# A gated linear-attention and GEGLU kernel: two neighbouring tokens in a partition instead of one

## The chip, the cores and the metric

The kernel runs on one core of a Trainium2 chip. The metric is the device time of one execution in microseconds (us). Five engines run their own instruction queues in order: PE (TensorE, matrix products), DVE (VectorE), ACT (ScalarE), POOL (GpSimd) and SP (SyncE, which here only issues transfers). PEld is PE's loading of weights, which the profile keeps apart. POOL issues transfers too, on a queue of its own (q0); SP's queue is q1. Sixteen DMA engines carry out the transfers of both.

## The reference

There are 4 batches of 8 heads, with 768 tokens of 48 elements, in fp32. For each batch and head a state `S` (48x48, complex) is carried from token to token: it is multiplied by a decay per row, and the outer product of `k` and `v` is added. `y` is `q` times the state's real part.

```
mag = sqrt(a_re^2 + a_im^2);  scale = min(mag, 0.999) / (mag + 1e-6)
for t in range(768):
    S = (a_re + i a_im)[t] * scale[t] * S  +  k[t] v[t]^T
    y[t] = q[t] . Re(S)
x = y as (3072 tokens, 384)
out = x + sigmoid(x @ w_res) * ((gelu(x @ w_gate) * (x @ w_val)) @ w_out)
```

The four weight matrices are 384x1536, 384x1536, 1536x384 and 384x384.

## The kernel before

The tokens are worked on in 12 groups `p` of 256 tokens: group p holds tokens 256*(p//4) to 256*(p//4)+255 of batch p%4, all heads. Groups 0 to 3 are the first of their batch, 8 to 11 the last. A group consists of two chunks `c` of 128 tokens. In every tile a partition is one token of a chunk, and the free dimension holds chunk, head and element (`wide = [128, C, H, D]`, L233). A load (`rows`, L282; `load`, L301) fetches one chunk of one input: 128 tokens x 8 heads x 48 elements, 192 KB in runs of 192 B.

**Gates** (`gates`, L306). A complex product of decays becomes a sum of log magnitudes and a sum of angles. ACT squares both parts (SQI, SQR), DVE adds and caps them (ADD), ACT takes the logarithm (LM); the tangent of the angle is formed (LNR, EXR, TH) and its arctangent taken (ATN). The running sums over the tokens of a chunk are fp32 products on PE with a triangular matrix of ones: CSL (L352) for log magnitudes, CST (L381) for angles, one per chunk and quantity, 128x384 each. Chunk 0 uses `lmat[0]`, which counts backwards from the end of chunk 0, and chunk 1 uses `lmat[1]`; so the midpoint of the group is the reference point. ACT makes E and Ei from CSL (EX, EI). The angle in turns is reduced to its fraction (OFF on ACT, FR on DVE L388), and ACT takes sine and cosine (SIN, COS; ABS on DVE before the cosine). The angle is carried on from chunk to chunk and from group to group: POOL multiplies the last row (CRA, CRB, L424) and an accumulating transfer adds it to the next chunk's first row (CDA, CDB, L429), ahead of that chunk's CST. For groups 4 to 11 small transfers bring decays to another layout (DR, DS, DE, DI, DT), of which ML, ME, MM, MN make the factor M.

**Products and attention** (L436, L458). DVE multiplies q with E and k with Ei (QE, KE, L441) and with the cosines and sines (QR, KR, L449) into the bf16 tiles `padQ` and `padK`. For groups 0 to 4 PE transposes them (TP, L481) and ACT and DVE copy the result out (CP); for groups 5 to 11 SP issues one transposing transfer per tile (QT, KT, L454). Per chunk and half of the heads, four products give the 128x128 attention blocks (AT), and DVE multiplies them with a triangular mask (AM). DK (L502) is padK times v, summed over the tokens of a chunk; MI and ED (L524 to L532) add it to the state `G`. Y (L540, L543) takes the masked blocks times v plus the query times the state. v is loaded as fp32 (Lvf, L615) and cast to bf16 by POOL (VC, L617).

**The feed-forward part** (`unit`, L556) runs on 7 units: groups 0, 1, then pairs (2,3) to (10,11). x is transposed (XT, XC), PE forms gate and value products (GP, VP, L569), ACT applies gelu (GE), DVE multiplies (HM, L575). RP (L579) and SG give the residual gate, OP (L589) is the output product, OT (DVE, L594) and RX (POOL, L600) finish it, and SP stores it (ST, L603).

**The order.** `ORDER` (L64) is one list of step names, written out. Each engine runs its steps in this order; semaphores hold a step until its operands are there. ACT must load a table before each change of function family (`log`, `trig`, `gelu` in the list). The weights are loaded by POOL with a cast to bf16 (Wg, Wv, Wr, Wo); two small copies, HOLDW and HOLDO (L627), keep them back until given `ai` loads have landed. The number of buffers of each tile is in `PARAMS` (L16).

Of the kernel before, what the change touches and what calls it, by code (L numbers as in the profile page):

```python
# [21 lines left out]
 'bufs': {'ar': 4,  # L22
# [3 lines left out]
          'k': 4,  # L26
          'vf': 2,
          'v': 4,
# [11 lines left out]
          'qk': 2,  # L40
          'atm': 2,
# [7 lines left out]
          'padK': 2},  # L49
 'share': {'kE': 'qE'},  # L50
 'sqe': {-1: ('ACT', 'ACT')},
 'offe': {-1: 'ACT'},
 'abse': {-1: 'DVE'},
 'cpe': ('ACT', 'DVE'),
# [3 lines left out]
 'holds': {'HOLDW': ('ai', 2, 1), 'HOLDO': ('ai', 4, 1)},  # L58
 'oph': 1,
 'rese': ['POOL'],  # L60
 'resl': 'POOL',
 'vhw': [0, 1, 2, 3, 4, 5, 6, 7, 8, 9, 10, 11]}

ORDER = """  # L64
Lar0.0 log Lk0.0 Lar0.1 Lar1.0 LNR0.0 Lar1.1 SQR0.0 EXR0.0 Lai0.0 LNR0.1 SQR0.1 Lai0.1 EXR0.1 Lai1.0 SQR1 Lai1.1
SQI0.0 ADD0.0 Lvf0.0 SQI0.1 TH0.0 LM0.0 Lq0.0 ADD0.1 CSL0.0 TH0.1 LM0.1 Lar2.0 SQI1 Lq0.1 CSL0.1 ADD1 EX0.0 VC0.0
EI0.0 Lq1.0 QE0.0 EX0.1 Lar2.1 EI0.1 DE0 trig Lar3.0 QE0.1 Lar3.1 ATN0.0 ATN0.1 Lvf0.1 CST0.0 SQR2 CST0.1 Lk0.1 OFF0.0
OFF0.1 FR0.0 Lk1.0 SQR3 FR0.1 Lk1.1 ABS0.0 SIN0.1 ABS0.1 CRB0 SIN0.0 VC0.1 Lai2.0 COS0.0 COS0.1 QR0.0 Lar4.0 QR0.1 log
Lai2.1 KE0.0 KE0.1 LNR1 Lai3.0 KR0.0 KR0.1 LM1 DK0.0 Lai3.1 EXR1 TP0.0.0 Lq1.1 MI0 SQI2 TH1 TP0.0.1 HOLDW Wr Lai4.0
# [12 lines left out]
FR3.0 Lar8.0 DK1.1 FR2.1 OFF3.1 Y1.1 ED1 CDB1 SIN2 Lq2.1 OP0.1.0 FR3.1 ATN4 CRB2 ABS2 Lai6.1 ABS3 CRB3 COS2 VC2.0
Lvf2.1 OT0.1 COS3 CDB0 KR2 Lai7.0 SIN3 RX0.1 QE2 Lai7.1 DK2.0 X1.1 XC1.0 XT1.1 MI2 Lar8.1 gelu XC1.1 VC2.1 QR2 GP1.0
Lq3.0 RP1.0 SQI6 KE3 DK2.1 Lq3.1 SG1.0 RP1.1 SQI7 ED2 VP1.0 Lq4.0 KR3 GE1.0 SG1.1 GP1.1 Lk4.0 SQR7 ADD6 GP1.2 GP1.3
Lq4.1 GE1.1 HM1.0 GE1.3 ADD7 DR6 GE1.2 GP1.4 SQR8 Lvf3.0 GP1.5 GP1.6 QE3 GE1.4 GP1.7 Lk4.1 DR7 GE1.5 GP1.8 GE1.6 GP1.9
QR3 GE1.7 GP1.10 Lai8.0 GE1.8 GP1.11 GE1.9 VP1.1 GE1.10 GE1.11 Lk5.0 VP1.2 HM1.1 VP1.3 log HM1.2 VC3.0 VP1.4 Lq5.0
HM1.3 VP1.5 HM1.4 VP1.6 HM1.5 VP1.7 LM4 Lq5.1 HM1.6 VP1.8 HM1.7 VP1.9 LM5 HM1.8 VP1.10 Lk5.1 HM1.9 VP1.11 ML4 HM1.10
LNR7 CSL4.0 Lai8.1 HM1.11 TP2.0.0 LNR6 TP2.0.1 Lk6.0 CP2.0.0.1 ME4 CSL4.1 ML5 EXR6 CP2.0.1.1 Lk6.1 DK3.0 CP2.0.0.0 TH6
ST0.0 EI4.0 AT2.0.0 Lvf3.1 ME5 MI3 EX4.0 DI4 CP2.0.1.0 AM2.0.0 CSL5.0 Lar9.0 EI4.1 TP2.1.0 EX4.1 KE4 AT2.0.1 EI5.0
CSL5.1 Lar9.1 DE4 EX5.0 AM2.0.1 CST4.0 CP2.1.0.0 ST0.1 CP2.1.0.1 Lq6.0 DI5 EX5.1 TP2.1.1 EI5.1 Y2.0 CP2.1.1.1 CST5.0  # L90
EXR7 DT4.0 Lar10.0 OP1.0.0 X2.0 TH7 DT4.1 OFF5.0 Lar10.1 OFF4.0 FR5.0 DE5 CP2.1.1.0 FR4.0 AT2.1.0 trig CRA5 Lq6.1
OT1.0 AT2.1.1 XT2.0 CRA4 OP1.1.0 AM2.1.0 DT5.0 AM2.1.1 XC2.0 Lq7.0 SQR9 MM4 CDA4 MN4 Lq7.1 EN4 ATN7 Y2.1 OT1.1 VC3.1
ATN6 TP3.0.0 DT5.1 Lk7.0 TP3.0.1 X2.1 CP3.0.0.1 DK3.1 CDB2 CP3.0.0.0 CP3.0.1.1 Lvf4.0 CST4.1 ED3 EB4 XT2.1 RX1.0
CP3.0.1.0 AT3.0.0 XC2.1 Lar11.0 TP3.1.0 SQR10 AM3.0.0 CDA5 AT3.0.1 CP3.1.0.1 OFF4.1 TP3.1.1 Lk7.1 AM3.0.1 CP3.1.0.0
RX1.1 CP3.1.1.1 Y3.0 CP3.1.1.0 Lk8.0 FR4.1 AT3.1.0 CDB3 X3.0 MM5 AT3.1.1 ABS4 CST5.1 SIN4 Lvf4.1 MN5 AM3.1.0 CRB4
XT3.0 COS4 Lk8.1 DS6.1 AM3.1.1 OFF5.1 EN5 Y3.1 VC4.0 Lai9.0 XC3.0 KR4 DS7.1 X3.1 ST1.0 SQI8 FR5.1 XT3.1 Lvf5.0 DK4.0
DS7.0 XC3.1 SIN5 ABS5 GP2.0 Lai9.1 VC4.1 KE5 COS5 GP2.1 DS6.0 MI4 GP2.2 gelu CRB5 KR5 Lvf5.1 GP2.3 ADD8 DK4.1 GE2.0
Lai10.0 GE2.3 GP2.4 VC5.0 ED4 GE2.1 Lai10.1 DR8 QE4 DK5.0 GE2.2 GP2.5 GE2.4 QR4 GP2.6 SQI9 VC5.1 KT5 GP2.7 QE5 GE2.5
GP2.8 GE2.6 ADD9 GE2.7 RP2.3 GE2.8 VP2.0 Lvf6.0 QR5 DR9 SG2.3 GP2.9 HM2.0 GP2.10 Lvf6.1 GE2.9 VP2.1 GE2.10 TP4.0.0
HM2.1 RP2.1 CP4.0.0.0 CP4.0.0.1 TP4.0.1 QT5 SG2.1 RP2.2 CP4.0.1.1 CP4.0.1.0 VC6.0 VP2.2 SG2.2 GP2.11 VC6.1 HM2.2  # L100
Lvf7.0 RP2.0 GE2.11 AT4.0.0 SG2.0 VP2.3 AM4.0.0 log Lk9.0 AT4.0.1 HM2.3 VP2.4 AM4.0.1 VP2.5 Lvf7.1 LM6 HM2.4 VP2.6 LM7
Lai11.0 HM2.5 VP2.7 HM2.6 VC7.0 LNR8 ST1.1 VP2.8 Lai11.1 HM2.7 LNR9 VP2.9 HM2.8 Lvf8.0 ML6 VP2.10 EXR8 VC7.1 HM2.9
VP2.11 EXR9 HM2.10 Lq8.0 Y4.0 HM2.11 ML7 ME6 CSL6.0 ME7 EB5 Lvf8.1 TH8 X4.0 CSL6.1 EI6.0 Lq8.1 TH9 TP4.1.0 EX6.0
TP4.1.1 DI6 EI6.1 Lq9.0 CP4.1.0.1 CSL7.0 EX6.1 KE6 CP4.1.0.0 CSL7.1 Lq9.1 DE6 CP4.1.1.0 CP4.1.1.1 CST6.0 EX7.0 Lar11.1
EX7.1 AT4.1.0 DT6.0 AT4.1.1 EI7.0 AM4.1.0 CST7.0 Lk9.1 EI7.1 DT6.1 AM4.1.1 OP2.0.0 OFF6.0 Lk10.0 OFF7.0 FR6.0 DI7 trig
FR7.0 CRA6 Lk10.1 Y4.1 OT2.0 CRA7 SQR11 XT4.0 AT5.0.0 MI5 CDA6 AT5.0.1 ATN8 OP2.1.0 AM5.0.0 CDA7 XC4.0 MM6 AM5.0.1
X4.1 MN6 DT7.0 ATN9 EN6 CST6.1 OT2.1 CDB4 Y5.0 OFF6.1 XT4.1 AT5.1.0 CDB5 EB6 XC4.1 AT5.1.1 OP2.2.0 FR6.1 X5.0 DT7.1
# [62 lines left out]
def kernel(  # L170
# [111 lines left out]
    def rows(a, p, c):  # L282
        s, b = divmod(p, B)
        t0 = (s * C + c) * 128
        return a[b, :, t0:t0 + 128, :].rearrange("h t d -> t h d")
# [411 lines left out]
```

## Time and profile before

| | |
|---|---|
| three runs | 302.81, 303.13, 304.01 us; median 303.13 |
| the profiled execution | 300.27 us, span of the instructions 298.5 us |
| busy | PE 242.7, ACT 216.4, DVE 209.3, PEld 148.4, POOL 126.5 us |
| loads of q, k, v, a_re, a_im | 120, of 192 KB; landing about 4 us after issue |
| moved by DMA | 39.98 MB in 164,891 packets; 156,800 of them under 512 B |
| ACT table loads | 21 of 1.28 us |

The span runs from the first to the last instruction of the profiled execution. "Busy" is the time in which an engine has an instruction in work; where two neighbours overlap, it counts once, so it is less than the number times the mean. A group of instructions is named by its line in the kernel, its engine and `output<-inputs`; many ACT steps share line 294, a helper. `A <- B` after an idle time says that A waited, and that B came last. "x2" in a chain counts instructions merged into one row; one fp32 product on PE appears as two MATMUL records.

### The profile page before, as it was taken

Reading aid. Unit: us, or ns where it says so; the run is one execution under the profiler, and the core shown is the slowest. Engines: PE = TensorE matmul, PEld = TensorE weight load, DVE = VectorE, ACT = ScalarE, POOL = GpSimd, SP = SyncE. Lnnn points to the kernel's source line nnn. Section 1 sums busy time; section 2 is a strip of 40 time slices with the busy share of each in tenths; the row PEclk is TensorE's granted clock in tenths of the full one; section 3 lists DMA queues with packets and bytes.
Section 4 is the critical chain, followed back from the end, with each engine's and each line's share of the span. In section 5 each row is a group of like instructions: output and inputs, shape, how many; then the busy total and the mean of one; then the engine's idle time right before and its main releaser. Section 6 shows DMA issues by size and latency. Waiting matters only on the chain.

```text
span 298.5 us, 5373 instructions
## 1 busy us (share of the span) xinstructions
PE 242.7 (81%) x1896; PEld 148.4 (50%) x1896; DVE 209.3 (70%) x352; ACT 216.4 (73%) x385; POOL 126.5 (42%) x164
## 2 busy tenths in 40 slices
PE   0327468965899877699987999969999899999992
PEld 0106236643586654355664446634557445664461
DVE  1448746659887759649879988889388898641721
ACT  5889988899799859579968789656695783347120
POOL 4225414068422969610799605990019420121013
PEclk9966879999599979799999999999999999999999
DMA  7999999999999996999418993297500197020002
GB/s 153 207 198 193 187 185 168 184 200 203 199 179 226 169 187 135 200 213 187 67 28 182 167 217 67 39 157 155 93 3 3 56 194 143 0 82 26 0 29 79
DMA packets 164891, 39.98 MB, mean 134 GB/s; under 512 B 156800, under 2 KB 164864, under 8 KB 164864
## 3 DMA queue, kind: packets, MB, share of 16 engines
q1 hardware_dynamic: 157376, 35.66, 60.5%
q0 software_dynamic: 7488, 3.97, 10.4%
q8 instruction: 15, 0.25, 0.3%
q14 instruction: 12, 0.10, 0.1%
HBM read 31.33 MB, written 4.76 MB: 121 GB/s over the span
## 4 chain that ended last, share of the span: by engine, by line
PE 57%; DMA 14%; DVE 8%; issue 6%; ACT 5%; SPq 5%; POOL 4%; POOLq 0%; DVEq 0%; ACTq 0%
PE gv L569 26%; PE sums L589 12%; DMA ai<-in_a_im_dram 8%; DMA d<-m 4%; SPq L304 4%; PE sums L579 4%; PE sums L381 3%; PE sums L352 3%; PE at L494 2%; PE dk L502 2%; PE tp L481 2%; DMA ar<-in_a_re_dram 1%; DVE atm L497 1%; ACT ar L294 1%; POOL m L342 1%
## 5 line engine op out<-in xcount | busy, mean ns | idle before, releaser
L575 DVE SCALAR_TENSOR_TENSOR h<-h,gv 128x512 bf16<-128x512 bf16 (+1 forms) x84 | 47.7, 607 | 20.8 <-PE gv L569 18.3
L569 PE MATMUL gv<-xT,wg 128*128 128x512 bf16 (+1 forms) x252 | 53.9, 360 | 6.2 <-ACT h L294 3.3
L294 ACT ACTIVATE h<-gv 128x512 bf16<-128x512 f32 (+1 forms) x84 | 41.6, 543 | 17.6 <-PE gv L569 16.5
L589 PE MATMUL sums<-wo,h 128*128 128x384 bf16 x288 | 50.6, 326 | 2.4 <-ACT Ei L294 2.4
L569 PE MATMUL gv<-xT,wv 128*128 128x512 bf16 (+1 forms) x252 | 52.5, 350 | 0.0
L600 POOL TENSOR_TENSOR ot<-ot,x 128x384 f32<-128x384 f32 x24 | 26.0, 1086 | 52.3 <-DVE ot L594 49.5
L569 PEld LDWEIGHTS <-wg 128*128 128x128 bf16 x252 | 25.1, 101 | 28.6 <-issue 7.9
L589 PEld LDWEIGHTS <-h 128*128 128x128 bf16 x288 | 27.4, 98 | 20.1 <-issue 2.3
L497 DVE TENSOR_TENSOR atm<-at,mask 128x512 bf16<-128x512 f32 x48 | 31.8, 683 | 5.2 <-PE at L494 4.9
L569 PEld LDWEIGHTS <-wv 128*128 128x128 bf16 x252 | 24.4, 98 | 20.5 <-issue 0.3
L424 POOL TENSOR_SCALAR G<-m 32x384 f32<-32x384 f32 x16 | 23.5, 1470 | 16.6 <-DVE m L388 13.1
L294 ACT ACTIVATE ar<-ar 128x768 f32<-128x768 f32 (+1 forms) x35 | 28.2, 819 | 2.0 <-DMA ar<-in_a_re_dram 1.9
L664 ACT ACT_TABLE_LOAD x21 | 26.9, 1283 | 1.1 <-PEq L681 0.7
L294 ACT ACTIVATE sg<-sums 128x384 f32<-128x384 f32 x24 | 11.7, 490 | 17.8 <-PE sums L579 17.6
L617 POOL CAST v<-vf 128x384 bf16<-128x384 f32 x24 | 17.5, 733 | 16.8 <-DMA vf<-in_v_dram 15.7
L594 DVE SCALAR_TENSOR_TENSOR ot<-sg,sums 128x384 f32<-128x384 f32 x24 | 13.2, 550 | 15.9 <-PE sums L589 12.3
L363 POOL DMA_DIRECT2D d<-Ei x8 | 4.0, 494 | 47.5 <-ACT Ei L294 40.1
L502 PE MATMUL dk<-v,padK 128*96 128x48 bf16 x160 | 11.0, 209 | 15.5 <-POOL v L617 7.2
L381 PE MATMUL sums<-ai,ut 128*128 128x384 f32 x40 | 17.7, 538 | 5.2 <-ACT qk L298 1.8
L294 ACT ACTIVATE m<-sums,magic 128x384 f32<-128x384 f32 x24 | 13.6, 584 | 11.0 <-PE sums L381 10.8
L502 PEld LDWEIGHTS <-padK 128*96 128x96 bf16 x160 | 10.5, 134 | 19.6 <-DVE padK L449 9.7
L352 PE MATMUL sums<-m,lt 128*128 128x384 f32 x24 | 11.3, 555 | 10.3 <-ACT m L294 10.3
(80 smaller groups left out, 478.0 us busy)
## 6 DMA issues: line engine op xcount, KB each, us to landing
ar<-in_a_re_dram SPq DMA_DIRECT2D x24, 192.0 KB, 4.2
k<-in_k_dram SPq DMA_DIRECT2D x24, 192.0 KB, 3.9
ai<-in_a_im_dram SPq DMA_DIRECT2D x24, 192.0 KB, 3.9
vf<-in_v_dram SPq DMA_DIRECT2D x24, 192.0 KB, 3.9
q<-in_q_dram SPq DMA_DIRECT2D x24, 192.0 KB, 4.1
out_dram<-ot SPq DMA_DIRECT2D x24, 192.0 KB, 2.3
wg<-in_moe_w_gate_dram POOLq DMA_DIRECT2D x4, 288.0 KB, 11.5
wv<-in_moe_w_val_dram POOLq DMA_DIRECT2D x4, 288.0 KB, 12.9
```

The costliest lines, as they stand in the source:

```text
L294: return nc.scalar.activation(out=out, in_=in_, func=func, **kw)
L352: st.add("CSL%d.%d" % (p, c), "PE", lambda c=c: nc.tensor.matmul(out=st["csl", (p, c)], lhsT=lmat[c], rhs=part(("m2", p), (c,)), start=Tru ...
L381: st.add("CST%d.%d" % (p, c), "PE", lambda c=c: nc.tensor.matmul(out=st["cst", (p, c)], lhsT=tmat[c if s == 0 else 1], rhs=part(("ai", p), ...
L424: st.add("CR%s%d" % (nm, p), "POOL", lambda: nc.gpsimd.tensor_scalar(out=row[96:128], in0=part(("m2", p), (c,))[96:128], scalar1=-2.0 * ma ...
L497: st.add("AM" + sfx, "DVE", lambda: nc.vector.tensor_tensor(out=st["atm", i], in0=st["at", i], in1=mask4, op=OP.mult), r=[("at", i)], w=[( ...
L502: return [nc.tensor.matmul(out=d[0:DD, h * D:(h + 1) * D], lhsT=K(c * H + h), rhs=st["v", p][:, c, h], start=(c == 0 and h == 0), stop=(h ...
L569: st.add("%sP%d.%d" % (nm.upper(), u, f), "PE", lambda f=f, nm=nm, w=w: [nc.tensor.matmul(out=st[nm + "p", (u, f)][:, 0:n], lhsT=w[:, i, f ...
L575: st.add("HM%d.%d" % (u, f), "DVE", lambda f=f: nc.vector.scalar_tensor_tensor(out=st["h2", u][:, f, 0:n], in0=st["h2", u][:, f, 0:n], sca ...
L589: st.add("OP%d.%d.%d" % (u, jj, hh), "PE", lambda jj=jj, fs=fs: [nc.tensor.matmul(out=st["op", (u, jj)], lhsT=st["h2", u][:, f, jj * 128:( ...
L600: st.add("RX%d.%d" % (u, jj), rese, lambda jj=jj, pc=(p, c), eng=eng: eng.tensor_tensor(out=st["ot", (u, jj)], in0=st["ot", (u, jj)], in1= ...
L617: st.add("VC%d.%d" % (p, c), "POOL", lambda c=c: nc.gpsimd.tensor_copy(out=st["v", p][:, c], in_=st["vf", (p, c)]), r=[("vf", (p, c))], w= ...
L664: nc.scalar.preload_act_table_set(tables[nm])
```

## The change

A partition now holds two neighbouring tokens, 2i and 2i+1, of the group's 256 (`wide = [128, H, C, D]`, where C is now the parity). It comes with these edits:

- **Loads.** One transfer per group and input (384 KB, runs of 384 B) instead of two; group 0 is loaded in halves of the heads, and its gate steps are split by heads. That makes 64 loads instead of 120.
- **Sums.** SL (POOL; DVE for group 0) adds the log magnitudes of the two tokens, one CSL per group sums the pairs, and the odd token's running sum is the result. UL (DVE) subtracts the odd token's own value, which gives the even token's. SP, CST and UT (DVE) do the same for the angles. The exponentials and OFF, FR still run once per parity. The lower half of `lmat` covers partitions 0 to 63, the upper 64 to 127, so the midpoint is kept.
- **Carry.** One row copy CR (DVE) and one accumulating transfer CD per group, for groups 0 to 3 to 4 to 7 and these to 8 to 11; none within a group.
- **Chunks.** Chunk c is now partitions 64c to 64c+63 with both parities, its 128 tokens in the order even, then odd. The mask is rebuilt for that order. The transposed tiles QT, KT are `[128, C, H*C, 64]`; the transposing transfer is one per chunk, of 64 partitions, 28 instead of 14.
- **v.** One load and one cast (VC, 128x768) per group into `vb`; VS (DVE, 64x768) copies chunk 0 for groups 0 to 7. Four transfers VX per group (48 in all, 64 partitions x 768 B, SP's queue) bring v into the even-odd order that Y needs (`vp`).
- **DK.** Groups 0 to 7: per half of the heads 8 products over both chunks, whose 96 columns hold the sum up to the midpoint and the whole sum. Groups 8 to 11: 16 products over 64 partitions. MI and ED are split by halves of the heads for groups 0 to 7.
- **Stores** take 128 rows that are two tokens apart in pairs of partitions; the rows stay 1,536 B.
- **Buffers.** `ar` 4 to 3, `k` 4 to 3, `atm` 2 to 6, `v` (4) gives way to `vb` (2) and `vp` (2), `qk` goes, PSUM stays.
- **Order.** The list is written anew. HOLDW and HOLDO wait for the loads of the same groups. The casts VC0 and VC1 stand ahead of the weights on POOL's queue, VC2 ahead of HOLDO.

Cut at the first gate product of each unit (GP0.0 to GP6.0), the two lists hold these numbers of steps (before/after):

| stretch | UL+UT | VS | CR | MI+ED | QE, QR, KE, KR | EN, MM, MN | CSL+CST | ATN | SIN+COS | tables | loads | VX | KT+QT |
|---|---|---|---|---|---|---|---|---|---|---|---|---|---|
| to GP0.0 | 0/6 | 0/2 | 1/2 | 2/4 | 9/9 | 0/0 | 8/6 | 5/5 | 4/6 | 4/4 | 31/22 | 0/5 | 0/0 |
| to GP1.0 | 0/4 | 0/2 | 3/2 | 3/4 | 7/4 | 0/0 | 8/4 | 2/0 | 6/2 | 4/3 | 23/14 | 0/7 | 0/0 |
| to GP2.0 | 0/4 | 0/2 | 3/1 | 3/9 | 6/11 | 6/6 | 8/4 | 2/4 | 3/6 | 2/3 | 33/15 | 0/12 | 0/0 |
| to GP3.0 | 0/4 | 0/1 | 5/1 | 4/7 | 9/8 | 5/2 | 8/4 | 2/2 | 5/4 | 3/3 | 22/7 | 0/4 | 3/6 |
| to GP4.0 | 0/4 | 0/1 | 2/2 | 4/8 | 8/7 | 7/8 | 8/4 | 2/2 | 4/4 | 3/4 | 11/6 | 0/8 | 4/8 |
| to GP5.0 | 0/4 | 0/0 | 2/0 | 2/2 | 8/9 | 6/7 | 8/4 | 0/0 | 4/4 | 4/3 | 0/0 | 0/12 | 4/9 |
| to GP6.0 | 0/0 | 0/0 | 0/0 | 2/2 | 5/4 | 0/1 | 0/0 | 0/0 | 0/0 | 1/1 | 0/0 | 0/0 | 3/5 |

The core of the diff:

```diff
- 'bufs': {'ar': 4,
+ 'bufs': {'ar': 3,
...
+ 'sle': {-1: 'POOL', 0: 'DVE'},
+ 'ste': {-1: 'POOL', 0: 'DVE'},
+ 'vce': {-1: 'POOL'},
+ 'vse': {-1: 'DVE'},
+ 'cre': 'DVE',
...
-    wide = [128, C, H, D]
+    wide = [128, H, C, D]
...
-    def rows(a, p, c):
+    def rows(a, p, h0=0, h1=H):
         s, b = divmod(p, B)
-        t0 = (s * C + c) * 128
-        return a[b, :, t0:t0 + 128, :].rearrange("h t d -> t h d")
+        t0 = s * C * 128
+        return a[b, h0:h1, t0:t0 + C * 128, :].rearrange("h (p r) d -> p h (r d)", r=C)
...
+        st.add("SL%d%s" % (p, z), sle, lambda: vec(sle).tensor_tensor(
+            out=Pc("m2", 0), in0=Pc("m2", 0), in1=Pc("m2", 1), op=OP.add),
...
+        st.add("CSL%d%s" % (p, z), "PE", lambda: nc.tensor.matmul(
+            out=summed(("csl", p), h), lhsT=lmat, rhs=Pc("m2", 0), start=True, stop=True),
...
+        st.add("UL%d%s" % (p, z), "DVE", lambda: nc.vector.tensor_tensor(
+            out=Pc("E", 0), in0=summed(("csl", p), h), in1=Pc("m2", 1), op=OP.subtract),
...
+        for c in (1, 0):
+            for nm, n, sc in (("EI", "Ei", -0.5), ("EX", "E", 0.5)):
+                src = [("csl", p, z)] if c else [("E", p, sub(z, 0))]
...
+        st.add("UT%d%s" % (p, z), "DVE", lambda: nc.vector.scalar_tensor_tensor(
+            out=Pc("ai", 0), in0=Pc("ai", 1), scalar=-I2PI, in1=summed(("cst", p), h), op0=OP.mult, op1=OP.add),
...
+            out=G[b][96:128], in0=st["m2", p][96:128, :, 1, :], scalar1=-2.0 * math.pi, scalar2=None, op0=OP.mult),
...
+                for c in range(C):
+                    st.add(nm.upper() + "T%d.%d" % (p, c), "SP", lambda nm=nm, c=c: nc.sync.dma_start_transpose(
+                        out=st[nm.upper() + "T", p][:, c], in_=st["pad" + nm.upper(), p][c * 64:c * 64 + 64]),
...
+            st.add("VS%d" % p, vse, lambda: copy(vse, st["vb", p][0:64, :, 0], st["vb", p][0:64, :, 1]),
...
+        for j in range(2 * C):
+            c, r = divmod(j, C)
+            st.add("VX%d.%d" % (p, j), "SP", lambda c=c, r=r: nc.sync.dma_start(
+                out=st["vp", p][r * 64:r * 64 + 64, c], in_=st["vb", p][c * 64:c * 64 + 64, r, 1]),
```

## The prediction

> **What bounds the kernel now.** I read the busy times by stretch first, cut at the start of the first gate product of each of the seven units (41.3, 77.2, 122.1, 160.7, 200.6, 238.0, 267.7 us). The columns are the length, then busy time of PE, PEld, DVE, ACT, POOL, the clock, the DMA share, GB/s.
>
> ```profile
> 0.00:41.30 41.30, 16.58 (x110) 10.08 (x111) 21.46 (x41) 33.89 (x56) 15.15 (x29) 0.79 1.06 187
> 41.30:77.20 35.90, 24.95 (x221) 17.82 (x221) 24.63 (x45) 33.08 (x57) 17.79 (x23) 0.97 1.12 190
> 77.20:122.10 44.90, 37.05 (x338) 27.04 (x339) 36.85 (x66) 37.74 (x72) 25.93 (x32) 0.91 0.94 182
> 122.10:160.70 38.60, 36.24 (x293) 21.40 (x292) 29.35 (x51) 30.26 (x55) 20.08 (x26) 0.96 0.69 133
> 160.70:200.60 39.90, 36.68 (x292) 21.41 (x291) 35.47 (x56) 31.04 (x58) 25.66 (x35) 1.00 0.75 135
> 200.60:238.00 37.40, 36.03 (x272) 20.56 (x272) 28.81 (x48) 26.67 (x50) 12.65 (x15) 1.00 0.34 69
> 238.00:267.70 29.70, 29.70 (x252) 17.28 (x251) 22.01 (x34) 14.63 (x25) 4.63 (x5) 1.00 0.48 105
> 267.70:298.50 30.80, 25.49 (x134) 12.83 (x131) 10.74 (x17) 9.12 (x16) 4.56 (x5) 0.98 0.09 33
> ```
>
> The reader is to see three regimes. Up to 77.2 us the DMA engines are full (1.06 and 1.12) and ACT is busy 66.97 of 77.2 us, 87%, while PE is half idle. From 77.2 to 238.0 us PE carries the kernel: 73.3 of 83.5 us in the first two stretches, 72.7 of 77.3 in the next two, and 94% over the three from 122.1 to 238.0 (108.95 of 115.9). DVE has room there: 66.2 and 64.3 us. From 238.0 on it is PE alone, and no gate work is left.
>
> Next the longest pieces of the chain that ended last, from 28 to 78 us (start, length, what):
>
> ```profile
> 29.44 19.43 DMA ai<-in_a_im_dram
> 49.17 0.83 POOL wo L641
> 51.46 9.73 DMA d<-m
> 64.22 3.13 DMA d<-m
> ```
>
> The first is one load of 192 KB that took 19.4 us because the weights and earlier loads stood before it; a held weight load and two tiny transfers follow on POOL's queue. So the start hangs on the DMA. The page's queue part gives the packets:
>
> ```profile
> q1 hardware_dynamic: 157376, 35.66, 60.5%
> q0 software_dynamic: 7488, 3.97, 10.4%
> HBM read 31.33 MB, written 4.76 MB: 121 GB/s over the span
> ```
>
> The 120 loads are 122,880 of the packets, 192 B each. Last, the groups by line (count, then busy us and mean ns) give prices:
>
> ```profile
> L600 POOL TENSOR_TENSOR ot<-ot,x 128x384 f32<-128x384 f32 x24 | 26.0, 1086 | 52.3 <-DVE ot L594 49.5
> L424 POOL TENSOR_SCALAR G<-m 32x384 f32<-32x384 f32 x16 | 23.5, 1470 | 16.6 <-DVE m L388 13.1
> L388 DVE SCALAR_TENSOR_TENSOR m<-m,sums 128x384 f32<-128x384 f32 x24 | 12.8, 547 | 7.8 <-ACT m L294 7.8
> L352 PE MATMUL sums<-m,lt 128*128 128x384 f32 x24 | 11.3, 555 | 10.3 <-ACT m L294 10.3
> ```
>
> **Part 1, loads of 384 B.** Packets fall from 122,880 to 61,440, for the same 23.6 MB. At 187 GB/s a 192 B packet costs an engine 16 x 192 B / 187 GB/s = 16.4 ns. A 384 B packet costs between 16.4 ns (bytes free) and 32.8 ns (packets free). The nearest other row is the weights: q0 took 10.4% of 16 x 298.5 us, 497 us; with some 2,500 tiny packets at 16 ns, its 4,992 weight packets of (31.33 - 23.6) MB / 4,992 = 1,549 B read took 91.5 ns each. A line through both points gives 16.4 + 192 x 75.1 / 1,357 = 27 ns, which I take as an estimate. All loads then need 61,440 x 27 / 16 = 104 us of the DMA instead of 126; bounds 63 and 126.
>
> The Trainium skill (DMA: Bandwidth & Descriptors, Why small descriptors are slow) charges each packet a fixed few cycles beside its bytes; that agrees in kind, and its count for unaligned pieces (9 + 3 cycles on average against 14 + 3) would make it 16.4 x 17 / 12 = 23 ns, and the loads 89 us. By that the start gains some 3 us more than below.
>
> The gain is only of use up to 77.2 us, where the DMA is full. ACT is next. By the counts of steps per stretch, ACT has some 3.3 us less to do ahead of the second unit's products, because two arctangents, parts of the sines and one table load now stand behind that point: 63.6 us. At 88% busy (87% now) the second unit starts at 63.6 / 0.88 = 72.3 us, **4.9 us earlier**; the chain from the ai load through POOL, above, loses a link because the casts of v stand ahead of the small transfers. If the DMA gives nothing, this term is 0.
>
> **Part 2, one sum per group and quantity.** Each group had two sums of log magnitudes and two of angles; now one each. A pair of the L352 records (one fp32 product) takes 0.65 to 0.70 us in the chain. 24 full-width products go: 24 x 0.66 = 15.8 us of PE, 5.3 of them in each of the two double stretches between 77.2 and 238.0 us. This is PE work that was on the path, but it only counts as long as PE stays the bound.
>
> **Part 3, what DVE and POOL take over.** New on DVE: UL and UT, one of each per group, 128x384 with a PSUM operand, like L388: 12 x 2 x 0.547 = 13.1 us. VS, 8 copies of 64x768 bf16: no row; the 128x384 copy of line 299 is 0.35 us, twice that is 0.70; I take 0.5, 4 us. CR, 8 of 32x384, between 0.35 (128x384, line 401) and 0.547: I take 0.35, 2.8 us. MI and ED in halves, 0.35 each where a whole was 0.55: +2.4. SL, SP of group 0: 4 x 0.35. In all 23.7 us; overlap between neighbours (the parts sum to 5% more than the busy time) makes it 22.6, and DVE goes **from 209.3 to 232 us**, past what PE will have (242.7 - 15.8 + DK, below = 229).
>
> By stretches, with the counts of steps before and after, DVE gains 11.4 us between 77.2 and 160.7 (8 UL/UT 4.4, 3 VS 1.5, 2 CR 0.7, MI/ED +1.75, four whole products moved in 4.1, three small ones out -1.1) and 7.3 between 160.7 and 238.0 (8 UL/UT 4.4, one VS 0.5, 2 CR 0.7, the rest 1.7). With the 5% off, DVE has 66.2 + 10.8 = 77.0 us and 64.3 + 6.9 = 71.2 us there, PE 73.3 - 5.3 = 68.0 and 72.7 - 5.3 = 67.4, ACT (some 3 us moved in) 71 and 58. **DVE becomes the bound.** Whether it can be filled as PE was is the question on which the sum rests. I take PE's 94%, as the busiest engine of an order fixed by hand: 77.0 / 0.94 = 81.9 us (83.5 before) and 71.2 / 0.94 = 75.7 us (77.3 before).
>
> POOL loses 16 row copies (L424, 23.5 us) and 8 accumulating transfers (8 us) and gains 22 adds like L600 (23.9 us): lighter by 8 us, not a bound. Its adds stand in the path of each sum, 1.1 us and a hop; the carry from chunk to chunk within a group (1.2 us on POOL, 2.8 us on the DMA and one more sum) is gone from the same path. I set one against the other.
>
> **Part 4, the rest.** DK: in the first 8 groups as many products, with 96 columns instead of 48 (a 128-column transpose pair of 8 takes 0.45 us, the 8 DK products 0.50: nothing; at most double, 8 us); in the last 4 groups 8 more of half depth, 4 x 8 x 0.06 = 2 us, half of it beside idle PE time. VX: 48 moves of 48 KB within SBUF, 2.4 MB, packets of 768 B: 48 x 64 x at most 55 ns / 16 = 11 us of DMA, spread over 230 us. They wait for the cast on SP's queue, with later loads, transposes and stores queued behind them; SP already waits 9.0 us for the casts' buffers and 85 us for results to store, mostly where loads run far ahead. Nothing, unless the loads come late. Fewer buffers for ar and k: the same answer. The transposes by DMA become 28 halves. Their DMA time was 60.5% of 298.5 us less 126 for loads and some 17 for stores, 38 us for 14. It stays if it goes by bytes, doubles if by instruction; from 122 us on the DMA is 0.09 to 0.75 busy, so it hides, and each pair may land some 2 us later (an issue takes 1.3 to 3.9 us of SP).
>
> Here the Trainium skill speaks against the change (the same page, Rules for kernel authors): two transfers to partition halves serialize, one of 128 partitions is better, and under 64 KB a transfer is mostly overhead. The page of before has no half transfers. By that rule the 14 transposes and 48 moves bring 62 overheads of some 2 us, 124 us in all; taken as latency beside other work they cost nothing, and one per unit on the path would cost 7 x 2 = 14 us.
>
> **The sum.** 72.3 + 81.9 + 75.7 + 29.7 + 30.8 = 290.4 us of span (the last two stretches unchanged, the 2 us of DK against DVE's 1 us less there). 300.27 - 298.5 = 1.8 us lie around it: 292.2 us, 97.3% of the profiled execution's 300.27. The median shown is 303.13, above that execution, so I scale: 303.13 x 0.973 = **295.0 us**.
>
> **Rivals.** (a) *The loads get no faster*, at 32.8 ns: the second unit starts at 77.2, the sum is 295.3 + 1.8 = 297.1, or 299.9 on the median's scale. For it: the DMA share is full with any packet size. Against: the weights' packets move bytes faster than the loads'. 16%, and from 298 to 304. (b) *DVE is no better filled than before*, **slower**: UL, UT, VS and CR stand in DVE's fixed order between the wide products, and whoever waits for them (ACT's exponentials of the even tokens, then PE) waits for everything ahead. The point that decides is 148.2 / 165.7 = 89% of DVE's time between the second unit's start and the sixth's (160.8 us now, 165.7 with the 4.9 added); below it the start's 4.9 us are given back. DVE's best stretch now is 35.47 of 39.9, 89% too. At 87%: 72.3 + 88.5 + 81.8 + 60.5 + 1.8 = 304.9, or 307.8 us. 28%. (c) *More comes out*: the short path without a carry, half as many PSUM sum tiles held, a packet at 23 ns: start at 69, DVE at 98%: 69 + 78.6 + 72.7 + 60.5 + 1.8 = 282.6, or 285.3 us. 13%. The forecast has 43%, from 290 to 300.
>
> **The numbers.** A measurement of this kernel can tell about 0.5%, 301.6 to 304.6 us. Faster: 41 of the forecast's 43, all 13 of (c), 8 of (a): 62%. Same: 2 + 7 + 3 of (b): 12%. Slower: the remaining 25 of (b) and 1 of (a): 26%. The range for 8 in 10 goes from (c)'s centre, a little lower, to (b)'s centre, a little higher: 284 to 309.
>
> **What would show it.** In the profile after: half the load packets and over 220 GB/s in the first stretch (step 1; at 190 it is wrong); second unit at 70 to 74 us; 24 pairs of fp32 sums and PE near 229 us; DVE at 230 or more and 92 to 95% busy between the second unit and the sixth. If DVE's total stays under 225, or it idles over 10% there behind ACT or POOL, part 3 is wrong. If AT products wait for KT or QT, or Y for vp, the hidden transfers were not hidden.

## The result and the profile after

The change made the kernel **slower**: 349.85 us (median of 4 runs, 348.56 to 351.49) against 303.57 us (4 runs, 302.81 to 307.73), a ratio of 1.154 with a 95% interval of 1.147 to 1.160. The forecast was 295.0 us. The execution profiled after has a span of 346.8 us. Ratios are taken over the fast executions of both kernels, and of the kernel before these are two of seven beside runs 1 to 8 (about 295 us) but nearly all beside runs 9 to 14 (about 299), so that steps between runs are read from medians here.

Busy time by stretch, cut again at the first gate product of each unit (now at 43.4, 71.7, 117.6, 162.0, 213.6, 262.7 and 305.9 us); the columns are those of the table of before.

```profile
0.00:43.40 43.40, 15.56 (x107) 11.10 (x108) 28.09 (x65) 35.51 (x63) 18.62 (x32) 0.89 1.07 225
43.40:71.70 28.30, 23.55 (x205) 17.49 (x206) 24.43 (x49) 26.47 (x50) 12.61 (x17) 0.86 1.06 236
71.70:117.60 45.90, 32.63 (x309) 23.47 (x310) 42.91 (x77) 40.77 (x73) 25.41 (x31) 0.83 0.67 172
117.60:162.00 44.40, 37.18 (x310) 22.36 (x308) 36.49 (x61) 34.09 (x60) 14.89 (x18) 0.92 0.61 103
162.00:213.60 51.60, 39.37 (x288) 22.17 (x288) 41.08 (x68) 31.89 (x58) 22.91 (x29) 0.86 0.64 112
213.60:262.70 49.10, 39.00 (x280) 21.99 (x281) 34.95 (x54) 26.76 (x50) 15.61 (x17) 0.88 0.49 63
262.70:305.90 43.20, 34.60 (x257) 19.10 (x258) 21.27 (x33) 13.43 (x24) 4.29 (x4) 0.84 0.50 71
305.90:346.80 40.90, 25.61 (x133) 12.81 (x131) 10.76 (x17) 9.13 (x16) 4.56 (x5) 0.85 0.10 36
```

The reader is to see that the start is what was forecast: 225 and 236 GB/s where it was 187 and 190, and the second unit at 71.7 us (forecast 72.3, before 77.2). The loss comes later: the fourth unit is 1.3 us late, the fifth 13.0, the sixth 24.7, the seventh 38.2, the end 48.3. (The third starts at 117.6 us. In the trace of before its first gate product starts at 115.0 us, and not at the 122.1 of the forecast's cut, so it is 2.6 us late and the start's 5.5 us are gone by then. The forecast's sum doesn't use that cut.) Neither PE (76 to 84% from 117.6 to 305.9 us) nor DVE (80 and 71% from 162 on) is full there, and the DMA share is 0.49 to 0.64 from 117.6 to 305.9 us. So something is waited for that fills none of these. The queue and the DMA issues on the page after:

```profile
q1 hardware_dynamic: 98992, 38.02, 53.6%
...
out_dram<-ot SPq DMA_DIRECT2D x24, 192.0 KB
```

The packets changed as meant: 61,440 fewer for the loads, 3,072 more for the moves of v. The list of waits of after names what PE stood for, and the chain that ended last has the same transfers in it:

```profile
DVE atm L536 <- PE at L533: 36.6, 14, 10.6
...
PE at L533 <- DMA QT<-padQ: 23.8, 8, 8.0
...
PEld L533 <- DMA out_dram<-ot: 8.3, 1, 8.3
...
DVE ot L645 <- DMA out_dram<-ot: 6.4, 3, 4.2
```

```profile
221.40 3.77 SPq L501
...
225.22 6.17 DMA QT<-padQ
...
233.63 0.92 SPq L501
...
234.60 4.21 DMA QT<-padQ
...
270.71 2.09 SPq L501
...
272.85 5.71 DMA QT<-padQ
...
327.40 6.46 DMA out_dram<-ot
```

PE waited 23.8 us for transposed q in 8 waits, up to 8.0 us each; the list of before has no wait for transposed q or k. A store is in the chain, and two of the waits are put down to stores. The 8.3 us of PEld end at the same moment, 277.7 us, as PE's 8.0 us for transposed q: they are one stall.

The packet records of the trace tell why. In the kernel before, a store's 128 packets of 1,536 B take 0.64 us in the commonest case, with 13 in flight in the mean; most stores are over in 0.6 to 1.3 us, four take 1.7 to 2.6. After, each store has about two in flight (2.1 in the mean) and takes 3.9 to 5.3 us; four in a row take 16.7 us. The view of the output, `(i r) d -> r i d` with r = 2, has an outermost dimension of 2. The records don't name the engine of a packet, but two in flight is what 2 of the 16 engines would carry, one packet each. The tail shows it in the DMA share (same columns): with hardly anything but stores under way it is 0.12, about 2 of 16.

```profile
300.00:320.00 20.00, 19.95 (x120) 10.17 (x119) 8.82 (x15) 6.97 (x14) 3.55 (x4) 1.00 0.12 41
```

The Trainium skill (DMA: Bandwidth & Descriptors, Rules for kernel authors) says just this: an outermost dimension under 16 confines the whole transfer to at most so many engines. The two in flight agree with it.

Who pays for it stands in the records too. The transposes' packets of 256 B took 121.6 ns in the mean where they started during a store, 26.1 elsewhere, the longest 4,992 ns, as long as a store. Load packets that started during a store took 23.6 ns, the others 24.4: the loads were not held up.

### The profile page after: what moved, and what is told of

Read it like the earlier page. It is cut to its first block, busy times and chain, and to the rows that moved or that the text cites. A ratio compares the mean times of both kernels' runs of the same rounds, so it can differ in the third digit from the quotient of the medians.

```text
span 346.8 us, 5358 instructions
## 1 busy us (share of the span) xinstructions
PE 247.5 (71%) x1884; PEld 150.5 (43%) x1884; DVE 240.0 (69%) x421; ACT 218.1 (63%) x391; POOL 118.9 (34%) x150
## 5 line engine op out<-in xcount | busy, mean ns | idle before, releaser
L620 PE MATMUL gv<-xT,wg 128*128 128x512 bf16 (+1 forms) x252 | 64.5, 409 | 7.8 <-DVE xT L322 7.2
L651 POOL TENSOR_TENSOR ot<-ot,x 128x384 f32<-128x384 f32 x24 | 26.6, 1108 | 71.2 <-DVE ot L645 68.5
L620 PEld LDWEIGHTS <-wg 128*128 128x128 bf16 x252 | 27.5, 113 | 35.7 <-issue 10.8
L533 PE MATMUL at<-QT,KT 96*128 96x128 bf16 x192 | 20.3, 238 | 29.9 <-DMA QT<-padQ 23.8
L533 PEld LDWEIGHTS <-KT 96*128 96x128 bf16 x192 | 15.1, 107 | 40.3 <-issue 22.5
L382 POOL TENSOR_TENSOR m<-m 128x384 f32<-128x384 f32 x11 | 10.9, 998 | 59.7 <-ACT m L317 59.7
L590 PE MATMUL y<-vp,atm 128*128 128x48 bf16 x192 | 14.4, 190 | 7.7 <-ACT x L321 3.9
L547 PE MATMUL dk<-vb,padK 128*96 128x96 bf16 x128 | 10.7, 240 | 12.6 <-DVE padK L496 9.3
L322 POOL CAST vb<-vf 128x768 bf16<-128x768 f32 x12 | 13.5, 1123 | 17.7 <-PE dk L547 6.7
L630 PE MATMUL sums<-wr,xT 128*128 128x384 bf16 x72 | 17.7, 375 | 2.6 <-DVE xT L322 2.6
L385 PE MATMUL sums<-m,lmat 128*128 128x384 f32 (+1 forms) x26 | 11.6, 550 | 10.0 <-ACT m L317 7.9
```

The lines of the kernel that those rows point to most:

```text
L322: return (nc.vector if eng == "DVE" else nc.gpsimd).tensor_copy(out=out, in_=in_)
L533: return [nc.tensor.matmul(out=st["at", i][:, j], lhsT=lhs("K", j % 2, g * 2 + j // 2), rhs=lhs("Q", j % 2, g * 2 + j // 2), start=True, s ...
L590: r.append(nc.tensor.matmul(out=ys, lhsT=st["atm", (p, h // 2)][:, h % 2 * 2 + c], rhs=st["vp", p][:, c, h], start=True, stop=first))
L620: st.add("%sP%d.%d" % (nm.upper(), u, f), "PE", lambda f=f, nm=nm, w=w: [nc.tensor.matmul(out=st[PN[nm], (u, f)][:, 0:n], lhsT=w[:, i, f * ...
L630: st.add("RP%d.%d" % (u, jj), "PE", lambda jj=jj: [nc.tensor.matmul(out=st["rp", (u, jj)], lhsT=st["xT", u][:, i, jj * 128:(jj + 1) * 128] ...
L651: st.add("RX%d.%d" % (u, jj), rese, lambda jj=jj, pc=(p, c), eng=eng: eng.tensor_tensor(out=st["ot", (u, jj)], in0=st["ot", (u, jj)], in1= ...
```

## The experiments

Every run was timed beside the kernel before on its chip, which took 298.5 to 299.7 us there. **Theory N**: the narrow stores hold two engines for 4 to 5 us at a time, and whatever shares them is late. **Theory H**: the halved transposes themselves. **Theory Q**: SP's in-order queue, in which moves of v and stores that wait hold back what is behind them. **Theory D**, the forecast's rival (b): DVE has too much to do.

**1. Wide stores.** The halves of a store are contiguous on the SBUF side, so that each store can be two transfers of 64 rows:

```
-  nc.sync.dma_start(out=out[...].rearrange("(i r) d -> r i d", r=C), in_=ot)
+  [nc.sync.dma_start(out=out[...].rearrange("(i r) d -> r i d", r=C)[r],
+                     in_=ot[r * 64:r * 64 + 64]) for r in range(C)]
```

> The changed kernel with each store issued as two, one per parity (64 partitions, rows of 1,536 B two rows apart), 48 stores instead of 24; nothing else. Theory N (narrow stores: the store's view has an outer dimension of 2, its 128 packets of 65 ns run on about 2 of the 16 DMA engines for 4 to 5 us, and the transposing transfers and later loads stand behind it on those engines): the stores go back to 1 to 2 us each, the last four land within some 3 us, and the AT products no longer wait for QT; 290 to 304 us. Theory H (halved transposes: twice as many transposing transfers, each as slow as a whole one): only the tail gains, 336 to 343 us. Theory D (DVE has too much in the new order): the same 336 to 343 us.

324.36 us (320.33 to 325.09), ratio 1.095 (1.077 to 1.114). The stores are wide again (9.5 of their packets in flight in the mean, mostly 0.9 to 1.5 us for the two transfers of a store), and on the page of this kernel they have a landing time like that of before:

```profile
out_dram<-ot SPq DMA_DIRECT2D x48, 96.0 KB, 2.2
```

Against 1.154 without this edit, the narrow stores cost 5.9 points of 299 us, some 18 us (21 by the medians: 1.154 x 299 = 345 against 324). N holds, but it is less than half of the loss, and the time expected under it was missed.

**2. Whole transposes alone.** Groups 5 to 11 transpose q and k by 14 whole transfers; the products then read blocks of other tokens, as many and as large.

```
-  for c in range(C): dma_start_transpose(out=QT[:, c], in_=pad[c * 64:c * 64 + 64])
+  dma_start_transpose(out=QT_flat, in_=pad)
```

> The changed kernel with 14 transposing transfers of 128 partitions instead of 28 of 64, at the place of the first half; the stores stay as they are. The attention blocks of groups 5 to 11 are then taken over the even and the odd tokens of all 128 partitions instead of over each half of the partitions, so that part of the computation is not the reference's; number and size of all products stay. Theory N: little, 335 to 350 us, since the whole transposes stand behind the same stores. Theory H: 300 to 318 us. Theory D: 340 to 350 us.

349.04 us (347.03 to 349.51), ratio 1.180 (1.167 to 1.194): nothing gained, as N has it. PE waited as long for transposed q as before the edit:

```profile
PE at L535 <- DMA QT<-padQ: 22.3, 4, 9.4
```

The packets of the whole transposes, too, took 124.6 ns in the mean during a store and 19.7 elsewhere.

**3. Both edits.**

> Both edits: 48 stores of 64 partitions and 14 whole transposes (attention blocks of groups 5 to 11 over other tokens, as in the run before). Theory N: within 4 us of the run with the stores alone, 288 to 302 us. Theory H: 290 to 300 us, far under the run with the stores alone. Theory D: 325 us or more.

312.30 us (309.50 to 314.35), ratio 1.054 (1.032 to 1.076). None of the three expectations held: N had 4 us for the transposes, H and N a time of 302 or less, D 325 or more. With wide stores the whole transposes are worth 12 us (324.36 to 312.30), which they were not in run 2. With whole transposes the wide stores are worth 37 us (349.04 to 312.30), where run 1 has some 20. So while one of the two is left it hides a part of what the other costs, and the share of each depends on which is taken off first. The waits of PE for q in run 1, then in run 3:

```profile
PE at L533 <- DMA QT<-padQ: 10.3, 6, 2.8
```

```profile
PE at L535 <- DMA QT<-padQ: 4.3, 3, 2.5
```

So 23.8 us of waiting became 10.3 and then 4.3. Some 13 us over the kernel before remain, and this kernel served as the base for the runs that look for them.

**4. The converse: the kernel before with the narrow view.** Only the output's view is changed.

```
-  out=out[t0:t0 + 128, :], in_=ot
+  out=out[t0:t0 + 128, :].rearrange("(i r) d -> r i d", r=C), in_=ot
```

> The kernel before with the changed kernel's view of the output in its 24 stores, nothing else: the same bytes in rows of 1,536 B, but to two sets of 64 rows (so the rows of each block of 128 come out permuted). Theory N: the stores take 4 to 5 us on 2 engines here too, and transposes and loads wait behind them: 318 to 345 us. Theories H and D: only the tail shows it, 303 to 313 us.

324.71 us (321.84 to 332.34), ratio 1.096 (1.072 to 1.120). One line that moves the same bytes in the same rows costs 26 us in the kernel before. N is shown from both sides.

**5. Without ABS (theory D), on run 3's kernel.** The cosine reads the signed turns through the sine table without its bias.

```
-  each("ABS", abse, ...)          # 12 x 952 ns of DVE
-  COS: act(o, ai, Sin, bias=hpi)
+  COS: act(o, m2, Sin, bias=0)
```

> The kernel with wide stores and whole transposes (312.3 us where the kernel before took 299.05), less one VectorE instruction per group: the cosine reads the signed turns through the sine table without its quarter-turn bias, so ABS (12 instructions, 952 ns each, 11.4 us of VectorE's 240.4) falls away; the output is not the reference's. Theory D: what is left of the loss is VectorE, which does 31 us more than in the kernel before and is the fullest engine from 45 to 242 us. Then most of 11 us of it shows: 303 to 308 us. Rival: what is left are waits on transfers and the lower granted clock, with VectorE only filling the time: 311 to 313.

305.01 us (304.37 to 307.43), ratio 1.037 (1.022 to 1.053): 7 us less than run 3, as D has it. (No execution of one run reaches into the range of the other; the intervals of the two ratios overlap.)

**6. Without the moves of v (theory Q), on run 3's kernel.** The 48 VX transfers are left out, and the products read `vb`.

> The kernel with wide stores and whole transposes (312.3 us), less the 48 moves that bring v into the chunks' order: the products of attention read v where it lies, in other tokens' order, so the output is not the reference's. Theory Q: SyncE's queue is in order, and a move that waits for its cast holds the transposes, stores and loads behind it: 303 to 308. Rival D (VectorE is what is left): 311 to 313, because nothing leaves VectorE.

305.39 us (301.45 to 308.19), ratio 1.027 (0.995 to 1.060): about 7 us less again, with a wide interval. D alone doesn't explain it.

**7. Loads in runs of 192 B, on run 3's kernel.** Each load is made as two, one for each parity.

```
-  dma_start(out=tile "p h (r d)", in_=rows)
+  for r in range(C): dma_start(out=tile[:, :, r], in_=rows[:, :, r * D:r * D + D])
```

> The kernel with wide stores and whole transposes (312.3 us), each load made as two DMAs of 192 B runs, one for each parity, so that the tile is filled the same but by the packets of the kernel before. If the longer runs bring what the prediction put on them (4.9 us by the second unit, and nothing later), this costs 3 to 6 us: 315 to 318. If loads are hidden once VectorE is the bound, 312; if the 60 more issues on SyncE's queue hold other transfers, over 320.

334.91 us (334.18 to 338.62), ratio 1.140 (1.121 to 1.159): 23 us more, far over the 3 to 6 that the forecast's own figure gives. Either the packets matter more than forecast, or the doubled issues do; run 12 tells which.

**8. The order on SP's queue, on run 1's kernel.** The moves VX7 and VX11 are put behind the transposes of q of groups 6 and 10.

> The changed kernel with wide stores (324.36 us) and its halved transposes, with one edit of the order on SyncE's queue: the four moves of groups 7 and 11 stand behind the two transposes of q of groups 6 and 10 and not between and ahead of them. Theory Q: the halves cost 12 us because of what stands ahead of them on the queue: 319 to 322. Rival: they cost it by their own issue time (1.2 to 2.5 us each) and their slower packets, wherever they stand: 323 to 326.

323.50 us (320.77 to 327.95), ratio 1.093 (1.058 to 1.127), where run 1 had 324.36: the same within their spreads. The rival holds here, that the halves cost by their own issue (1.75 us each, median, where a whole one takes 2.4 to 3.2) and packets, wherever they stand.

**9. The moves of v issued by GpSimd, on run 1's kernel.** They follow their cast on the engine that makes it.

```
-  st.add("VX...", "SP", lambda: nc.sync.dma_start(...
+  st.add("VX...", "POOL", lambda: nc.gpsimd.dma_start(...
```

> The changed kernel with wide stores (324.36 us), with the 48 moves of v issued by GpSimd right behind its own cast and no longer by SyncE. Theory Q: what the moves cost (about 7 us: 312.3 to 305.39 without them) is that they stand on SyncE's queue ahead of transposes, stores and loads: 316 to 320. Rival: their cost is their packets or v's later arrival, wherever they are issued: 323 to 326. If their issue on GpSimd delays what GpSimd feeds, over 326.

317.41 us (315.76 to 318.08), ratio 1.064 (1.056 to 1.071). The same moves on another queue give 7 us back, as much as leaving them out did in run 6 (there with whole transposes). Their cost is their place on SP's queue, and not their bytes. PE's waits for q fall with it, from 10.3 to 5.7 us. For the moves, then, Q holds; what the halves cost is another question (run 11).

**10. Without ABS and without the moves of v, on run 3's kernel.**

> The kernel with wide stores and whole transposes (312.3 us), less both the 48 moves of v and the 12 ABS of VectorE; the output is not the reference's. Alone each took 7 us off. If the two are separate parts of what is left, they add up: 297 to 300, the time of the kernel before. If they only shorten the same wait, 303 to 306.

297.76 us (295.36 to 300.77), ratio 0.994 (0.989 to 0.999). The two cuts add up, 7.3 and 6.9 alone, 14.5 together. With them the kernel is where the kernel before is.

**11. The kernel before with halved transposes.**

```
-  dma_start_transpose(out=QT, in_=padQ)
+  [dma_start_transpose(out=QT[:, :, c * 64:c * 64 + 64], in_=padQ[c * 64:c * 64 + 64]) for c in range(C)]
```

> The kernel before with one edit: each of its 14 transposing DMAs made as two of 64 partitions, which fill the same tile. If the halves cost by their own issue time (1.8 us each where a whole one takes 2.3 to 3.2) and packets, the 12 us of the changed kernel show here too: 306 to 312. If they cost only behind the moves and stores of the changed order: 299 to 302.

301.44 us (299.44 to 303.43), ratio 1.011 (1.003 to 1.018). The halves cost 2.4 us there, and 12 us in the changed kernel. Their issue times and landings are alike in both (1.75 to 1.78 us and 4.3 us, medians), and so are the 256 B packets (27.9 and 28.2 ns mean, against 22 to 24 of whole transposes). So their own issue and packets alone don't make 12 us. Nor do the moves ahead of them on SP's queue: run 9 (halves, moves on GpSimd's queue) and run 6 (whole, no moves) are 12 us apart as well (317.41 and 305.39), and PE's waits for q in these two, first run 9, then run 6, differ as much as those of runs 1 and 3:

```profile
PE at L533 <- DMA QT<-padQ: 5.7, 5, 1.5
```

```profile
PE at L535 <- DMA QT<-padQ: 0.2, 1, 0.2
```

H is real, and apart from Q. Why it costs 12 us in the changed kernel and 2.4 in the kernel before stays open; in the latter PE waits for transposed q only once, 1.0 us, even with halves.

**12. Loads in two halves of the heads, on run 3's kernel.** As many issues as in run 7, with 384 B packets.

> The kernel with wide stores and whole transposes (312.3 us), each load made as two DMAs of half the heads: as many issues as with 192 B runs (334.91 us), but packets of 384 B. If the 23 us of the short runs were the doubled issues on SyncE: 330 to 336. If they were the packets: 311 to 315. Something between splits them.

313.98 us (313.58 to 316.39), ratio 1.054 (1.047 to 1.061). The issues cost 1.7 us, within the spread of run 3; the packets of run 7 the other 21. In the first 20 us, run 12, then run 7 (columns as above):

```profile
0.00:20.00 20.00, 3.63 (x8) 2.13 (x8) 9.60 (x29) 14.16 (x28) 7.55 (x19) 1.00 0.86 218
```

```profile
0.00:20.00 20.00, 3.63 (x8) 2.14 (x8) 7.66 (x25) 12.30 (x24) 6.68 (x17) 1.00 0.93 179
```

218 against 179 GB/s, and the second unit starts at 74.5 against 83.2 us.

**13. Less on DVE, with the change's own result, on run 9's kernel.** VS and CR go to GpSimd (`'vse': 'POOL'`, `'cre': 'POOL'`).

> The changed kernel with wide stores and the moves of v issued by GpSimd (317.41 us), with VS (8 copies, 2.8 us in all) and CR (8 scalings, 3.3 us in all) moved from VectorE to GpSimd: the lightest form with the change's own output that these runs point to. Theory D: VectorE's time shows in part, as ABS did (7 us of time for 11.4 us of VectorE): 6 us less on it give 312 to 315. Rival: GpSimd's slower copy comes later on a chain of waits and gives it back: 317 to 320.

323.91 us (322.13 to 324.52), ratio 1.083 (1.076 to 1.089): 6.5 us slower than run 9, over both expectations. DVE's busy time hardly fell, 241.3 to 240.1 us, though 6 us of work had left it: GpSimd went from 148.0 to 167.9 us, and DVE's other instructions took longer in sum. Whether the time was lost there or behind GpSimd's own longer queue was not separated. Runs 13 and 15 belong together.

**14. Control: the kernel before without ABS.**

> The control: the kernel before (299.03 us), less its ABS (729 ns per group, 8.7 us of VectorE's 209.3) as in the run without ABS; the output is not the reference's. Theory D says that VectorE became the bound by the change, so that here the same cut gives little: 297 to 300. Rival: the cut shortens the chain from turns to rotation, or VectorE was already the bound, in either kernel: 291 to 294, and then the 7 us say nothing of what the change added.

295.98 us (293.42 to 299.44), ratio 0.988 (0.981 to 0.996): 2.5 us, between the two expectations, where run 5 had 7.3. DVE's busy time fell by 6.6 us here (209.3 to 202.7) and by 7.6 in run 5 (240.4 to 232.8). So a cut of DVE shows to 38% in the kernel before and nearly whole in the changed one, as D has it, though the executions of runs 3 and 14 lie 5 and 6 us apart, wide for such shares; that the whole 7 us come of the change is not shown.

**15. The pair sums by TensorE, on run 9's kernel.** Two fp32 products add up in PSUM as before; GpSimd's SL and SP fall away.

```
-  SL, SP: tensor_tensor(out=m2[c=0], in0=m2[c=0], in1=m2[c=1], op=add)
-  matmul(out=csl, lhsT=lmat, rhs=m2[c=0], start=True, stop=True)
+  [matmul(out=csl, lhsT=lmat, rhs=m2[c], start=(c == 0), stop=(c == 1)) for c in range(C)]
```

> The changed kernel with wide stores and the moves of v issued by GpSimd (317.41 us), with the pair sums taken back: each sum is two fp32 products that add up in PSUM, as in the kernel before, and GpSimd's two pair additions per group fall away. TensorE gets 24 products of some 0.55 us more (13 us), GpSimd loses 24 additions of 1.0 to 1.15 us (26 us). The prediction put the 15.8 us of TensorE down as the change's gain, hidden where VectorE is the bound. If TensorE's time shows: 324 to 330. If it is hidden under VectorE: 316 to 319. If the additions stood in the chain to the gates and slowed VectorE's own instructions: 308 to 314.

322.82 us (321.74 to 323.34), 5.4 us more than run 9, between the times expected. PE's busy time rose by 17.9 us (242.0 to 259.9), and some third of it shows. At the same time DVE fell from 241.3 to 231.1 us, though only SL and SP of group 0 (four at 0.35 us) had left it. The same lines in run 9, then in run 15:

```profile
L536 DVE TENSOR_TENSOR atm<-at,mask 128x512 bf16<-128x512 f32 x48 | 32.1, 683 | 13.3 <-PE at L533 13.3
L487 DVE TENSOR_TENSOR kE<-k,Ei 128x768 bf16<-128x768 f32 x11 | 13.4, 1220 | 0.1
L552 DVE TENSOR_TENSOR G<-G,M 96x384 f32<-96x384 f32 x8 | 8.2, 1029 | 0.0
```

```profile
L536 DVE TENSOR_TENSOR atm<-at,mask 128x512 bf16<-128x512 f32 x48 | 32.1, 684 | 18.7 <-PE at L533 18.5
L487 DVE TENSOR_TENSOR kE<-k,Ei 128x768 bf16<-128x768 f32 x11 | 10.8, 982 | 0.1
L552 DVE TENSOR_TENSOR G<-G,M 96x384 f32<-96x384 f32 x8 | 5.9, 739 | 0.0
```

The instruction that reads a product from PSUM keeps its 683 ns; these two with both inputs in SBUF take a fifth and more less here. Not all do (`ai<-ar,ai` went from 997 to 1,110 ns), because a mean mixes two kinds: `G<-G,M` took 538 to 548 ns or 1,001 and more in each of these runs and in the changed kernel, never between. Of the 84 instructions of seven kinds that read SBUF alone (`G<-G,M`, kE, qE, padQ, padK, `ai<-ar,ai` and FR of the even tokens), 19 took over 5% more than the shortest of their form in run 9, 19 in the changed kernel and 8 in run 15. GpSimd was at work during every one of them, and during most of the short ones too.

**16. The stores issued by GpSimd too, on run 15's kernel.**

> The kernel of the run with products for the pair sums, with the stores issued by GpSimd too, right behind its own residual additions: on SyncE's queue they waited 88 us for those additions, ahead of transposes and loads. Theory Q: 3 to 8 us less than the run with products for the pair sums. Rival: the waits end in time for what stands behind them: the same within 2 us, or longer by what the issues hold GpSimd.

317.68 us (315.63 to 318.74), 5.1 us less than run 15, by Q. SP had waited 88.5 us in 18 waits for results to store in run 9 (`SPq L654 <- POOL ot L651: 88.5, 18, 25.2`), with transposes and loads behind them.

No form with the change's own result came near the kernel before; the best are runs 9 and 16, 6% over it. Whole transposes that leave the chunks apart weren't tried.

## Why the prediction was wrong

**Part 1, right.** 61,440 load packets, 225 GB/s and more, second unit at 71.7 us for 72.3. A 384 B packet took 24.4 ns (mean of the packet records), the forecast's estimate was 27; the 23 ns that it worked out from the Trainium skill's page came nearer. Rival (a) is out. Against the kernel before, the second unit starts 5.5 us earlier. Runs 7 and 12 show what the long runs are worth in the changed order: 21 us, 8.7 of them by the second unit's start (83.2 against 74.5 us). That is not a gain over the kernel before, whose order starts this unit at 77.2 us with short runs; it shows that in the new order loads were not hidden later either.

**Part 2, the products gone, the gain mostly hidden.** Run 15 shows 5.4 us for both sums, not 15.8. The products were gone: the fp32 sums took 44.1 us of PE before and 23.1 after, 21 less. But the rest of PE's work rose by 25.8 us, to 247.5 in all (229 forecast). The mean granted clock fell from 0.946 to 0.869, and the same 252 gate records took 360 ns before and 409 after, 10.6 us together; the other 15 us were not taken apart.

**Part 3, mis-sized.** DVE has 240.0 us, not 232. The added instructions had the forecast's prices where they read PSUM (UL and UT 0.55 us); the excess lies in what the forecast left at its old price. `G<-G,M` and the int32 step (ABS) got slower, and half of FR reads SBUF where all of it read PSUM before, 818 ns for the 547 that were kept in the sum; these three make 8.6 us. Two rows of before, then those of after, FR in its two forms:

```profile
L401 DVE TENSOR_SCALAR ai<-m 128x768 int32<-128x768 int32 x11 | 7.9, 729 | 0.2
L509 DVE TENSOR_TENSOR G<-G,M 96x384 f32<-96x384 f32 x8 | 5.2, 647 | 0.2
```

```profile
L430 DVE TENSOR_SCALAR ai<-m 128x768 int32<-128x768 int32 x11 | 10.5, 952 | 0.1
L419 DVE SCALAR_TENSOR_TENSOR m<-m,ai 128x384 f32<-128x384 f32 x11 | 8.9, 818 | 0.1
L552 DVE TENSOR_TENSOR G<-G,M 96x384 f32<-96x384 f32 x8 | 8.3, 1042 | 0.0
...
L419 DVE SCALAR_TENSOR_TENSOR m<-m,sums 128x384 f32<-128x384 f32 x11 | 5.9, 547 | 0.9 <-ACT m L317 0.9
```

Between the second and sixth unit DVE was filled to 81% (155.4 of 191.0 us), under rival (b)'s point of 89%. But (b)'s mechanism, DVE's fixed order, is not what did it: with stores and transposes out of the way (run 3) the same order filled DVE to 91.5% (154.1 of 168.5 us from 73.6 to 242.1; from the second unit's start on, columns as above):

```profile
73.60:160.00 86.40, 70.87 (x615) 47.25 (x620) 78.63 (x137) 74.11 (x133) 38.81 (x48) 0.86 0.59 143
160.00:203.00 43.00, 36.75 (x286) 21.21 (x290) 40.84 (x68) 32.03 (x58) 23.89 (x29) 0.94 0.67 142
203.00:242.10 39.10, 35.49 (x277) 20.46 (x280) 34.62 (x55) 26.58 (x50) 15.73 (x17) 0.97 0.44 75
242.10:275.00 32.90, 30.29 (x244) 17.21 (x247) 20.48 (x32) 13.48 (x24) 3.38 (x3) 0.95 0.43 85
275.00:307.70 32.70, 27.12 (x142) 13.89 (x142) 11.64 (x19) 9.12 (x16) 5.47 (x6) 0.95 0.18 43
```

(b) had the sign, for the most part by other causes than its own, and its 307.8 us are 42 short.

**Part 4, the step that failed.** It took the stores as some 17 us of DMA and gave their new view no price at all: the rows stay 1,536 B, and bytes and row length were all that was looked at. Which engines carry a transfer was not asked. That is some 20 us with halved transposes (run 1), 37 with whole ones (runs 2 and 3), 26 in the kernel before (run 4). The forecast kept the last two stretches at 60.5 us; they took 84.1, and 65.6 in run 3. Of the transposes it said "so it hides, and each pair may land some 2 us later"; in the changed order they were on PE's path: 12 us (run 3), against 2.4 in the kernel before (run 11). Of the moves of v it said "Nothing, unless the loads come late"; they cost 7 us as a place in SP's queue (runs 6 and 9). PE's waits for transposed q fell by 4.6 us when they left it (run 9); whether late loads have a part was not separated. The 14 us that were weighed against the halves, with one overhead per unit on the path, are near the measured 12, but no run shows that the 12 come of one overhead per unit. Of the forecast's last test one half came true: AT waited for QT; no wait of PE for `vp` is in the list.

**The account**, as steps of the median: 345 us (1.154 x 299) with everything; less 21 with wide stores (324); less 12 with whole transposes (312); less 7 without the moves of v (305); less 7 for ABS, which stands for DVE's added work (298). The order of the steps sets the shares of the first two. The 298 are the time of the kernel before, with work left out that the change needs, so the gain of the longer loads and of the fewer sums is used up inside them. What it went into, term by term (UL, UT, the slower SBUF instructions, the lower clock, fewer buffers, the new order), was not separated and stays open.

## What to carry to other kernels

When a change touches a DMA's view, look at its outermost dimension before its run length: the same rows in the same bytes cost 26 us in run 4, with two packets in flight in place of some 13. A transfer that is cheap by its bytes still has a place in an in-order queue, and what stands behind it (here the transposes that PE needs next) pays when it waits; issuing it on the engine that makes the data gave 7 us back (run 9). Before two experiments are read, put the loudest fault right: with narrow stores the whole transposes looked worthless, without them they were worth 12 us.

## What the runs showed of the hardware

- A transfer between SBUF and DRAM whose DRAM side had an outermost dimension of 2 had about two packets in flight (2.1 in the mean); each store of 196,608 B took 3.9 to 5.3 us, where most took 0.6 to 1.3 before. Packets of DMA transposes that started meanwhile took 121.6 ns in the mean, against 26.1; load packets were not slower.
- Load packets of 384 B took 24.4 ns in the mean, those of 192 B 16.5: twice the bytes for 1.5 times the time.
- VectorE instructions whose inputs all lie in SBUF are slower at times while GpSimd works: `G<-G,M` took 1,042 ns in the mean after, 1,029 in run 9 and 739 in run 15, where GpSimd's pair additions were gone, while instructions with a PSUM input kept 547 and 683 ns. All long cases had GpSimd at work beside them (run 15). The Trainium skill (GPSIMD Engine Reference, 1. Specifications) states this contention for instructions with two SBUF inputs; these rows agree. Moving 6 us of work from VectorE to GpSimd (run 13) took 1.2 us off VectorE's busy time.
- The mean granted clock was mostly lower where PE was busy for less of the span: 0.946 at 81% before, 0.906 at 78% in run 3, 0.869 at 71% after. Run 15, with 0.903 at 81%, and run 7, with 0.923 at 74%, don't fit.
